# Steps 3 and 1 of a convolution kernel alternate in batches of four units in place of two, over all eight PSUM banks

## The chip, the cores and the metric

The kernel runs on one core of one Trainium2 chip. The metric is the device time of one execution in microseconds. A core has TensorE (matmuls, written PE; its weight loads are written PEld), VectorE (DVE), ScalarE (ACT), GpSimd (POOL) and SyncE (SP), which issues most DMAs. Matmuls write to PSUM, which the kernel uses as eight banks of 128 x 512 float32; ScalarE and VectorE copy or combine from there into SBUF.

## The reference

Two parts follow each other: a long convolution with a gate, and a soft mixture of experts over its output. The change lies in the convolution.

```python
def _attn_ref(x, v, pos_emb, w1, w2):          # x, v: (4, 11456, 128)
    h_filt = (np.maximum(pos_emb @ w1, 0.0) @ w2) * np.exp(-0.01 * pos)[:, None]
    u = x * v
    L = 2 * S
    Uf = np.fft.rfft(u, n=L, axis=1)
    Hf = np.fft.rfft(h_filt, n=L, axis=0)
    y = np.fft.irfft(Uf * Hf[None], n=L, axis=1)[:, :S, :]
    return x * y

def _moe_ref(x, phi, w1, w2):                  # x: the 45824 rows of the above
    logits = x @ phi                           # 8 experts x 4 slots
    d = softmax of logits over the rows;  slot_input = d.T @ x
    slot_out = relu(slot_input[e] @ w1[e]) @ w2[e]     for each expert e
    c = softmax of logits over the slots
    return c @ slot_out
```

## The kernel before

The transforms are done as matmuls with tables of cosines and sines, of length 111 x 197 in place of 2 x 11456. The 128 channels are cut into eight groups of 16 (`G = 8`, index `g`), and the 64 sequences of a group into 16 units of four (`NU = 16`, index `u`). A group goes through four steps:

- Step 1 (`first`, `first_out`): VectorE forms a unit's folded products of x and v (`p1_sd`, five instructions, in the place of the loaded x), TensorE multiplies them with `tab1x` on four quarters of its array at once (L138), and ScalarE copies two banks per unit into the tile `T` (L150).
- Step 2 (`p2`): matmuls of `T` with `W` into one bank (L279), a product with the filter's spectrum `Hs` on VectorE (L282), two sums on GpSimd back into `T`.
- Step 3 (`p3`): eight matmuls per unit of `T` with `tab3` (L296; the trace has two records for each), two banks per unit, and two ScalarE copies into the tile `E` (L302).
- Step 4 (`p4`, `p4_copy`, `p4_gate`, `p4_out`): matmuls of `E` with `tab4` into two banks (L331), two ScalarE copies, VectorE's sums and the gate with x, and DMAs to the scratch tensor.

The loop over `g` overlaps two groups. For `g` from 1 to 7 an iteration has two stages: first step 3 of group `g - 1` and step 1 of group `g` alternate, unit by unit; then step 4 of group `g - 1` and step 2 of group `g` do. Step 1 of a pair of units writes the part of `T` that step 3 of the same pair reads, so step 3 of a pair comes first. `inorder` and `steady` keep each engine's instructions in the order in which the code is written.

In the first stage (L385 to L412) the pairs `b` = 0 to 7 go: step 3 of units 2b and 2b + 1, then step 1 of the same units. In the first pair alone the matmuls of step 1 come ahead of step 3, and their copies behind. So step 3 of pairs 0 and 1 stand side by side, and step 1 of pairs 0 and 1 at the two sides of them. After each step 3 unit VectorE's `p1_sd` of the unit two further on is queued; after each step 1 unit the load of x six units further on (`p1_x`, into the place that this unit leaves, `ld` has 6). `p1_v` loads v. From the fourth pair on, loads of `Hs` for step 2 are put between.

PSUM is two pools of four banks. `psa` has four buffers of one bank, handed out in turn: step 1 takes two for a unit, step 2 one for each four columns. `pso` (tag `psb`) has two buffers of two banks: step 3 takes one for a unit, step 4 one for a block of rows. A buffer is taken again only when what was in it has been read.

```python
psa = ctx.enter_context(tc.tile_pool(name="psa", bufs=4, space=bass.MemoryType.PSUM))
pso.append(ctx.enter_context(tc.tile_pool(name="pso", bufs=2, space=bass.MemoryType.PSUM)))
```

Of the kernel before, what the change touches and what calls it, by code (L numbers as in the profile page):

```python
# [11 lines left out]
F32 = mybir.dt.float32  # L12
F32R = mybir.dt.float32r
AF = mybir.ActivationFunctionType
# [7 lines left out]
J = 99  # L22
# [3 lines left out]
R = 56  # L26
RP = 64
FO = 64
G = 8
# [32 lines left out]
def conv_part(ctx, tc, cp, moe, xf, vf, xi, xe, pos, w1, w2, win, t1x, t1h, wt, t3, t4, hs, scr):  # L62
# [64 lines left out]
        eng.tensor_tensor(out=hid[:, 0, rs], in0=hb[:, :, 0], in1=hb[:, :, 1], op=ALU.add)  # L127
        nc.vector.tensor_tensor(out=hid[:, 1, rs], in0=hb[:, :, 0], in1=hb[:, :, 1], op=ALU.subtract)

    def first(g, u, sd):  # L130

        ps = [psa.tile([128, 2, 2, J], F32, tag="psa", name=f"p1_{g}_{u}_{h}") for h in range(2)]
        for i in range(2):
            for s in range(2):
                for h in range(2):
                    js = slice(RP * h, RP * h + JH)
                    for d in range(2):
                        steady(g, nc.tensor.matmul(  # L138
                            ps[h][RP * d : RP * d + RP, i, s, :], lhsT=sd[js, i, s, d, :],
                            rhs=tab1x[js, J * (s + d) : J * (s + d + 1)],  # L140
                            start=True, stop=True, tile_position=(RP * h, RP * d)))
        return ps

    def first_out(g, u, ps):

        for h in range(2):
            dst = T[:, :, 2 * (u % 2) + h, u // 2]
            src = ps[h].rearrange("p c s k -> p s k c")
            if g or h == 0:
                steady(g, nc.scalar.activation(dst, src, AF.Copy))  # L150
            else:
                inorder(nc.vector.tensor_copy(out=dst, in_=src))
# [51 lines left out]
    def p1_v(g, u):  # L204
        k = u % HV if g == 0 else u - PRE
        if 0 <= k < HV:
            vt = Hs.rearrange("p k x -> p (k x)")[:, 8 * R * k : 8 * R * k + 8 * R]
        elif HV <= k < NU - 3:
            vt = m_half(g, k - HV)[:, : 8 * R]
        else:  # L210
            vt = ld.tile([128, 8 * R], F32, tag="lv", name=f"v_{g}_{u}", bufs=2)
        vt = vt.rearrange("p (c q r) -> p c q r", c=2, q=4)
        inorder(nc.sync.dma_start(out=vt, in_=vf[g, u]))
        vts[u] = vt

    def p1_x(g, u):
        if g == 0 and u < NU // 2:
            xt = moe.E[:, J * N1 + 8 * RP * u :][:, : 8 * RP].rearrange("p (c q r) -> p c q r", c=2, q=4)
        elif g == 0 and u >= NU - 2:
            xt = m_half(g, u).rearrange("p (c q r) -> p c q r", c=2, q=4)  # L220
        else:
            xt = ld.tile([128, 2, 4, RP], F32, tag="ld", name=f"x_{g}_{u}")
        inorder(nc.sync.dma_start(out=xt, in_=xf[g, u]))
        xts[u] = xt

    def p1_sd(g, u, eng):
        xt, vt = xts.pop(u), vts.pop(u)
        xr = xt[:, :, :, :R]
        inorder(eng.tensor_tensor(out=xr, in0=xr, in1=vt, op=ALU.mult))  # L229
        for m, op in ((0, ALU.add), (2, ALU.subtract)):  # L230
            inorder(eng.tensor_tensor(out=vt[:, :, m : m + 2], in0=xr[:, :, 0:2], in1=xr[:, :, 2:4], op=op))
        sd = xt.rearrange("p c (s d) r -> p c s d r", s=2)
        vq = vt.rearrange("p c (s q) r -> p c s q r", s=2)
        for d, op in ((0, ALU.add), (1, ALU.subtract)):
            inorder(eng.tensor_tensor(out=sd[:, :, :, d, :R], in0=vq[:, :, :, 0], in1=vq[:, :, :, 1],
                                      op=op))
        return sd
# [30 lines left out]
    for k in range(0, J, 4):  # L268
        filter_second(k)

    def p1(g, u, sd):
        first_out(g, u, first(g, u, sd))

    def p2(g, k0):
        n = min(KB, J - k0)
# [11 lines left out]
        inorder(nc.gpsimd.tensor_tensor(out=Ty[:, 0], in0=m[:, :n, 0, 0], in1=m[:, :n, 1, 1], op=ALU.subtract))  # L287
        inorder(nc.gpsimd.tensor_tensor(out=Ty[:, 1], in0=m[:, :n, 1, 0], in1=m[:, :n, 0, 1], op=ALU.add))  # L288

    def p3(g, u):  # L290
        ps = pso[0].tile([J, 2, 512], F32, tag="psb", name=f"p3_{g}_{u}")
        for k in range(2):
            pk = ps[:, k, : 8 * R].rearrange("p (i q r) -> p i q r", i=2, q=4)
            for i in range(2):
                for s in range(2):
                    inorder(nc.tensor.matmul(pk[:, i, 2 * s : 2 * s + 2, :].rearrange("p q r -> p (q r)"),  # L296
                                             lhsT=T[0:N1, s, 2 * k + i, u // 2, :, u % 2],
                                             rhs=tab3[:, 2 * R * s : 2 * R * (s + 1)],
                                             start=True, stop=True))
        for k in range(2):  # L300
            c = 4 * u + 2 * k
            inorder(nc.scalar.activation(  # L302
                E[:J, :, :, c : c + 2].rearrange("p r q c -> p q r c"),
                ps[:, k, : 8 * R].rearrange("p (i q r) -> p q r i", i=2, q=4), AF.Copy))

    AINV = pow(N1, -1, N2)

# [71 lines left out]
    for g in range(G + 1):  # L379

        if g == 0:
            for u in range(NU):
                p1(g, u, sds.pop(u))
        elif g < G:
            if not pso:  # L385
                first_ps.close()
                pso.append(ctx.enter_context(tc.tile_pool(name="pso", bufs=2, space=bass.MemoryType.PSUM)))
            for b in range(NU // 2):
                if b >= 4:
                    for k in range(11 * (2 * b - 8), min(J, 11 * (2 * b - 5 if b == 7 else 2 * b - 6)), 11):  # L390
                        inorder(nc.sync.dma_start(out=Hs[:, k : k + 11], in_=hs[g, :, k : k + 11]))
                us = (2 * b, 2 * b + 1)
                ps = {u: first(g, u, sds[u]) for u in us if b == 0}
                for u in us:
                    p3(g - 1, u)
                    if u + 2 < NU:
                        sds[u + 2] = p1_sd(g, u + 2, nc.vector)
                for u in us:
                    if b:
                        ps[u] = first(g, u, sds[u])  # L400
                    first_out(g, u, ps[u])
                    w = u + 6
                    if w < NU:
                        p1_x(g, w)
                    elif w < NU + PRE and g + 1 < G:
                        p1_x(g + 1, w - NU)
                if b == 0:
                    for w in range(PRE + HV, NU):
                        p1_v(g, w)
                if b == NU // 2 - 1 and g + 1 < G:  # L410
                    for w in range(PRE):
                        p1_v(g + 1, w)  # L412
        else:
            dead = moe.E[:, 8 * 4 * C : 16 * 4 * C]
            spare = ([sm.tile([128, PW], F32, tag="m", name=f"xl_{i}", bufs=3) for i in range(3)]
                     + [spare[i % 2] for i in (next(turns), next(turns))]
                     + [dead[:, PW * i : PW * i + PW] for i in range(2)])
            turns = count()
            xvs = [p4_load(g - 1, rb) for rb in ORDER[:5]]
            moe.weights()  # L420
            for u in range(NU):
                p3(g - 1, u)
            moe.places()
# [611 lines left out]
```

## Time and profile before

| | us |
|---|---|
| median of 3 runs (lowest, highest) | 955.26 (954.97, 956.76) |
| the profiled execution | 958.19 |
| its span, first to last instruction | 956.4 |
| TensorE busy in the span | 906.3 (95%) |
| TensorE weight loads busy | 818.2 (86%) |
| VectorE busy | 735.1 (77%) |
| ScalarE busy | 445.7 (47%) |
| GpSimd busy | 382.0 (40%) |
| mean granted TensorE clock | 0.977 |

An engine is busy while at least one of its instructions runs. Rows of the timeline give start, length, engine, line, operation, operands and count, and in brackets the idle time ahead of the row and what ended it; rows of the stretches give the busy time of each engine with the count of instructions, then the granted TensorE clock, the share of the DMA engines and GB/s. Names lose their numbers in the trace: `p` stands for the PSUM tiles of steps 1 to 4, so the line tells which step it is. Matmuls overlap: a record lasts about 0.26 us in step 3, while one starts every tenth of a microsecond. Seven of the eight groups (`g` = 1 to 7) have the stage that the change touches, of some 38 us each; group 4 lies at 391 to 475 us.

### The profile page before, as it was taken

Reading aid. Unit: us, or ns where it says so; the run is one execution under the profiler, and the core shown is the slowest. Engines: PE = TensorE matmul, PEld = TensorE weight load, DVE = VectorE, ACT = ScalarE, POOL = GpSimd, SP = SyncE. Lnnn points to the kernel's source line nnn. Section 1 sums busy time; section 2 is a strip of 40 time slices with the busy share of each in tenths; the row PEclk is TensorE's granted clock in tenths of the full one; section 3 lists DMA queues with packets and bytes.
Section 4 is the critical chain, followed back from the end, with each engine's and each line's share of the span. In section 5 each row is a group of like instructions: output and inputs, shape, how many; then the busy total and the mean of one; then the engine's idle time right before and its main releaser. Section 6 shows DMA issues by size and latency. Waiting matters only on the chain.

```text
span 956.4 us, 32999 instructions
## 1 busy us (share of the span) xinstructions
PE 906.3 (95%) x14042; PEld 818.2 (86%) x14042; DVE 735.1 (77%) x1282; ACT 445.7 (47%) x965; POOL 382.0 (40%) x582
## 2 busy tenths in 40 slices
PE   6999999999999999999999999999999979997992
PEld 6998989999999999999999999999999967774541
DVE  7936768699789879979978997998693248886671
ACT  0655437514711741571174157117414438885461
POOL 4001760292077028207702820760382007778700
PEclk9899999999999999999999999999999989999995
DMA  8923985457735735873573576457247787774499
GB/s 254 397 72 119 336 267 169 140 168 245 229 123 171 247 120 172 247 233 118 157 255 122 173 236 212 148 171 245 84 131 243 226 287 272 262 262 115 193 416 377
DMA packets 104239, 201.18 MB, mean 210 GB/s; under 512 B 14167, under 2 KB 65577, under 8 KB 100252
## 3 DMA queue, kind: packets, MB, share of 16 engines
q1 hardware_dynamic: 103806, 198.89, 63.0%
q8 instruction: 111, 1.82, 0.8%
q14 instruction: 36, 0.29, 0.1%
q10 hardware_dynamic: 254, 0.11, 0.0%
q0 software_dynamic: 32, 0.07, 0.0%
HBM read 139.12 MB, written 59.90 MB: 208 GB/s over the span
## 4 chain that ended last, share of the span: by engine, by line
PE 81%; POOL 6%; DMA 5%; ACT 2%; issue 2%; DVE 2%; SPq 0%; DVEq 0%; ACTq 0%
PE p L296 22%; PE p L279 19%; PE p L331 17%; PE p L138 10%; PE f L160 3%; PE f L170 2%; DMA hs<-E 2%; PE pw L875 2%; POOL E L654 2%; POOL hs L664 2%; DMA out_dram<-xreg 2%; PE fl L181 1%; POOL hs L662 1%; PE pt L559 1%; PE ct L730 1%
## 5 line engine op out<-in xcount | busy, mean ns | idle before, releaser
L287 POOL TENSOR_TENSOR T<-m 111x256 f32<-111x256 f32 (+1 forms) x200 | 147.4, 737 | 424.5 <-DVE m L282 424.5
L282 DVE TENSOR_TENSOR m<-p,T 111x1024 f32<-111x1024 f32 (+1 forms) x175 | 200.0, 1205 | 25.1 <-PE p L279 24.0
L296 PE MATMUL p<-tab,T 111*99 111x112 f32 x2048 | 212.1, 263 | 2.6 <-DVE E L356 1.6
L296 PEld LDWEIGHTS p<-tab,T 111*99 111x99 f32 x2048 | 201.8, 171 | 10.7 <-issue 2.7
L279 PE MATMUL p<-T,W 128*111 128x128 f32 x1584 | 194.7, 278 | 0.0
L279 PEld LDWEIGHTS p<-T,W 128*111 128x111 f32 x1584 | 183.0, 173 | 7.3
L340 ACT ACTIVATE vc<-p 128x416 f32<-128x416 f32 x112 | 51.8, 515 | 285.3 <-DVE p L345 192.5
L331 PE MATMUL p<-tab,E 99*64 99x104 f32 x3584 | 173.4, 254 | 1.8 <-ACT E L302 1.1
L331 PEld LDWEIGHTS p<-tab,E 99*64 99x64 f32 x3584 | 162.6, 137 | 9.7 <-issue 1.3
L302 ACT ACTIVATE E<-p 99x448 f32<-99x448 f32 x256 | 130.2, 574 | 84.9 <-PE p L296 84.9
L288 POOL TENSOR_TENSOR T<-m 111x256 f32<-111x256 f32 (+1 forms) x200 | 145.9, 730 | 0.0
L150 ACT ACTIVATE T<-p 128x396 f32<-128x396 f32 x240 | 102.3, 529 | 6.3 <-PE p L138 6.1
L138 PE MATMUL p<-tab1x,x 53*64 53x99 f32 x3776 | 96.4, 248 | 3.1 <-DVE m L282 1.6
L138 PEld LDWEIGHTS p<-tab1x,x 53*64 53x64 f32 x3776 | 84.5, 132 | 9.9 <-DVE m L282 1.8
L345 DVE TENSOR_TENSOR p<-p,vc 128x832 f32<-128x832 f32 x56 | 57.3, 1023 | 22.0 <-ACT vc L340 22.0
L560 ACT ACTIVATE xreg<-pt 128x512 f32<-128x512 f32 x90 | 48.4, 598 | 9.1 <-PE pt L559 8.9
L559 PE MATMUL pt<-ident,xreg 128*128 128x128 f32 x358 | 48.8, 281 | 3.8 <-DMA xreg<-scr 3.8
L654 POOL TENSOR_TENSOR E<-lt,mx 128x512 f32<-128x512 f32 (+1 forms) x23 | 23.6, 1026 | 65.0 <-ACT et L636 65.0
L229 DVE TENSOR_TENSOR x<-x,T 128x448 f32<-128x448 f32 x55 | 34.0, 619 | 19.5 <-DMA x<-in_xf_dram 15.1
L559 PEld LDWEIGHTS pt<-ident,xreg 128*128 128x128 f32 x358 | 40.8, 148 | 9.1 <-DMA xreg<-scr 4.0
L353 DVE TENSOR_TENSOR E<-p,E 128x824 f32<-128x824 f32 x46 | 46.8, 1016 | 1.6
L282 DVE TENSOR_TENSOR m<-p,E 111x1024 f32<-111x1024 f32 (+1 forms) x25 | 29.0, 1207 | 18.9 <-ACT E L186 12.9
(107 smaller groups left out, 973.6 us busy)
## 6 DMA issues: line engine op xcount, KB each, us to landing
x<-in_xf_dram SPq DMA_DIRECT2D x118, 256.0 KB, 4.5
out_dram<-xreg SPq DMA_DIRECT2D x21, 1024.0 KB, 12.8
E<-in_xi_dram SPq DMA_DIRECT2D x46, 412.0 KB, 3.6
scr<-E SPq DMA_DIRECT2D x84, 206.0 KB, 3.2
T<-in_vf_dram SPq DMA_DIRECT2D x65, 224.0 KB, 5.1
hs<-E SPq DMA_DIRECT2D x12, 1024.0 KB, 5.0
T<-hs SPq DMA_DIRECT2D x63, 176.0 KB, 3.5
mv<-in_vf_dram SPq DMA_DIRECT2D x42, 224.0 KB, 5.3
```

The costliest lines, as they stand in the source:

```text
L138: steady(g, nc.tensor.matmul(ps[h][RP * d : RP * d + RP, i, s, :], lhsT=sd[js, i, s, d, :], rhs=tab1x[js, J * (s + d) : J * (s + d + 1)], ...
L150: steady(g, nc.scalar.activation(dst, src, AF.Copy))
L279: steady(g, nc.tensor.matmul(ps[:, i].rearrange("p b c -> p (b c)"), lhsT=W[:, k0 + i, :], rhs=Tf[:, :, k0 + i, :], start=True, stop=True))
L282: inorder(nc.vector.tensor_mul(m[:, :n].rearrange("p k s e c i -> p k s (e c i)").rearrange("p k s (b c) -> p k s b c", c=CG), ps[:, :n].u ...
L287: inorder(nc.gpsimd.tensor_tensor(out=Ty[:, 0], in0=m[:, :n, 0, 0], in1=m[:, :n, 1, 1], op=ALU.subtract))
L288: inorder(nc.gpsimd.tensor_tensor(out=Ty[:, 1], in0=m[:, :n, 1, 0], in1=m[:, :n, 0, 1], op=ALU.add))
L296: inorder(nc.tensor.matmul(pk[:, i, 2 * s : 2 * s + 2, :].rearrange("p q r -> p (q r)"), lhsT=T[0:N1, s, 2 * k + i, u // 2, :, u % 2], rhs ...
L302: inorder(nc.scalar.activation(E[:J, :, :, c : c + 2].rearrange("p r q c -> p q r c"), ps[:, k, : 8 * R].rearrange("p (i q r) -> p q r i", ...
L331: inorder(nc.tensor.matmul(pv[RP * h : RP * h + RP, 2 * k + i, w, :], lhsT=E[:J, r, 2 - 2 * w + s, :], rhs=tab4[:, s, o : o + NJ], start=( ...
L340: inorder(nc.scalar.activation(vc[:, w], pv[:, :, 0, :], AF.Copy, scale=2.0 * w - 1.0))
L345: inorder(nc.vector.tensor_tensor(out=pw, in0=pw[:, 1:2].to_broadcast([128, 2, 4, NJ]), in1=vc, op=ALU.add))
L559: inorder(nc.tensor.transpose(pt[:, j, :], self.xt[i][:, k + j, :], self.ident))
```

## The change

Steps 3 and 1 now alternate in batches of four units. The units 0 to 3 keep their beginning: step 1's matmuls of units 0 and 1, step 3 of 0 and 1, their copies; then step 3 of 2 and 3 and step 1 of 2 and 3. Batches 1 to 3 are step 3 of four units, then step 1 of the same four. A new function `banks` gives either step two banks from either pool: one double buffer of `pso` (`large`), or two single ones of `psa`. Step 3 takes single ones for the first two units of a batch and a double one for each of the last two. Step 1 does the same, except that in the last batch it is the first two units that take the double ones. In the first four units step 3 takes double, double, single, single; step 1 single, single, double, double. The loads of `Hs` go out four ahead of batch 2's step 3 and five ahead of batch 3's, in place of two to three ahead of each of the last four pairs. VectorE keeps its order (`p1_sd`), and so do the loads of x and v among each other on SP.

```diff
--- before.py
+++ after.py
@@ -127,9 +127,15 @@
         eng.tensor_tensor(out=hid[:, 0, rs], in0=hb[:, :, 0], in1=hb[:, :, 1], op=ALU.add)
         nc.vector.tensor_tensor(out=hid[:, 1, rs], in0=hb[:, :, 0], in1=hb[:, :, 1], op=ALU.subtract)
 
-    def first(g, u, sd):
-
-        ps = [psa.tile([128, 2, 2, J], F32, tag="psa", name=f"p1_{g}_{u}_{h}") for h in range(2)]
+    def banks(g, u, name, large):
+        if large:
+            t = pso[0].tile([128, 2, 512], F32, tag="psb", name=f"{name}_{g}_{u}")
+            return [t[:, h] for h in range(2)]
+        return [psa.tile([128, 512], F32, tag="psa", name=f"{name}_{g}_{u}_{h}") for h in range(2)]
+
+    def first(g, u, sd, large=False):
+
+        ps = [t[:, : 4 * J].rearrange("p (c s k) -> p c s k", c=2, s=2) for t in banks(g, u, "p1", large)]
         for i in range(2):
             for s in range(2):
                 for h in range(2):
@@ -268,8 +274,8 @@
     for k in range(0, J, 4):
         filter_second(k)
 
-    def p1(g, u, sd):
-        first_out(g, u, first(g, u, sd))
+    def p1(g, u, sd, large=False):
+        first_out(g, u, first(g, u, sd, large))
 
     def p2(g, k0):
         n = min(KB, J - k0)
@@ -287,10 +293,10 @@
         inorder(nc.gpsimd.tensor_tensor(out=Ty[:, 0], in0=m[:, :n, 0, 0], in1=m[:, :n, 1, 1], op=ALU.subtract))
         inorder(nc.gpsimd.tensor_tensor(out=Ty[:, 1], in0=m[:, :n, 1, 0], in1=m[:, :n, 0, 1], op=ALU.add))
 
-    def p3(g, u):
-        ps = pso[0].tile([J, 2, 512], F32, tag="psb", name=f"p3_{g}_{u}")
+    def p3(g, u, large=True):
+        ps = [t[:J, : 8 * R] for t in banks(g, u, "p3", large)]
         for k in range(2):
-            pk = ps[:, k, : 8 * R].rearrange("p (i q r) -> p i q r", i=2, q=4)
+            pk = ps[k].rearrange("p (i q r) -> p i q r", i=2, q=4)
             for i in range(2):
                 for s in range(2):
                     inorder(nc.tensor.matmul(pk[:, i, 2 * s : 2 * s + 2, :].rearrange("p q r -> p (q r)"),
@@ -301,7 +307,7 @@
             c = 4 * u + 2 * k
             inorder(nc.scalar.activation(
                 E[:J, :, :, c : c + 2].rearrange("p r q c -> p q r c"),
-                ps[:, k, : 8 * R].rearrange("p (i q r) -> p q r i", i=2, q=4), AF.Copy))
+                ps[k].rearrange("p (i q r) -> p q r i", i=2, q=4), AF.Copy))
 
     AINV = pow(N1, -1, N2)
 
@@ -385,31 +391,45 @@
             if not pso:
                 first_ps.close()
                 pso.append(ctx.enter_context(tc.tile_pool(name="pso", bufs=2, space=bass.MemoryType.PSUM)))
-            for b in range(NU // 2):
-                if b >= 4:
-                    for k in range(11 * (2 * b - 8), min(J, 11 * (2 * b - 5 if b == 7 else 2 * b - 6)), 11):
-                        inorder(nc.sync.dma_start(out=Hs[:, k : k + 11], in_=hs[g, :, k : k + 11]))
-                us = (2 * b, 2 * b + 1)
-                ps = {u: first(g, u, sds[u]) for u in us if b == 0}
-                for u in us:
-                    p3(g - 1, u)
+            def third(us, larges):
+                for u, large in zip(us, larges):
+                    p3(g - 1, u, large)
                     if u + 2 < NU:
                         sds[u + 2] = p1_sd(g, u + 2, nc.vector)
+
+            def behind(u):
+                w = u + 6
+                if w < NU:
+                    p1_x(g, w)
+                elif w < NU + PRE and g + 1 < G:
+                    p1_x(g + 1, w - NU)
+
+            def spectrum(i0, i1):
+                for k in range(11 * i0, 11 * i1, 11):
+                    inorder(nc.sync.dma_start(out=Hs[:, k : k + 11], in_=hs[g, :, k : k + 11]))
+
+            ps = [first(g, u, sds[u]) for u in range(2)]
+            third(range(2), (True, True))
+            for u in range(2):
+                first_out(g, u, ps[u])
+                behind(u)
+            for w in range(PRE + HV, NU):
+                p1_v(g, w)
+            third(range(2, 4), (False, False))
+            for u in range(2, 4):
+                p1(g, u, sds[u], True)
+                behind(u)
+            for b in range(1, NU // 4):
+                if b > 1:
+                    spectrum(4 * b - 8, 5 * b - 6)
+                us = range(4 * b, 4 * b + 4)
+                third(us, (False, False, True, True))
                 for u in us:
-                    if b:
-                        ps[u] = first(g, u, sds[u])
-                    first_out(g, u, ps[u])
-                    w = u + 6
-                    if w < NU:
-                        p1_x(g, w)
-                    elif w < NU + PRE and g + 1 < G:
-                        p1_x(g + 1, w - NU)
-                if b == 0:
-                    for w in range(PRE + HV, NU):
-                        p1_v(g, w)
-                if b == NU // 2 - 1 and g + 1 < G:
-                    for w in range(PRE):
-                        p1_v(g + 1, w)
+                    p1(g, u, sds[u], (u % 4 < 2) if b == 3 else (u % 4 > 1))
+                    behind(u)
+            if g + 1 < G:
+                for w in range(PRE):
+                    p1_v(g + 1, w)
         else:
             dead = moe.E[:, 8 * 4 * C : 16 * 4 * C]
             spare = ([sm.tile([128, PW], F32, tag="m", name=f"xl_{i}", bufs=3) for i in range(3)]
```

How the change moves instructions on TensorE at the start of the stage, for `g` = 1; `p1_1_u` is step 1 of group 1, unit u (a further 0 or 1 is a single bank), `p3_0_u` step 3 of group 0, unit u. Before, from the last row of step 1's unit 1:

```order
L138 MATMUL p1_1_1_1_1624<-tab1x_74,x_1_1_1037 64x99 x2
L296 MATMUL p3_0_0_1641<-tab3_75,T_78 99x112 x8
L296 MATMUL p3_0_1_1657<-tab3_75,T_78 99x112 x8
L296 MATMUL p3_0_2_1692<-tab3_75,T_78 99x112 x8
L296 MATMUL p3_0_3_1708<-tab3_75,T_78 99x112 x8
L138 MATMUL p1_1_2_0_1724<-tab1x_74,x_1_2_1180 64x99 x2
L138 MATMUL p1_1_2_1_1725<-tab1x_74,x_1_2_1180 64x99 x2
```

Step 3 of units 0 to 3 goes through the two double buffers twice. In the change:

```order
L302 MATMUL p3_0_0_1641<-tab3_75,T_78 99x112 x8
L302 MATMUL p3_0_1_1657<-tab3_75,T_78 99x112 x8
L302 MATMUL p3_0_2_0_1692<-tab3_75,T_78 99x112 x4
L302 MATMUL p3_0_2_1_1693<-tab3_75,T_78 99x112 x4
L302 MATMUL p3_0_3_0_1709<-tab3_75,T_78 99x112 x4
L302 MATMUL p3_0_3_1_1710<-tab3_75,T_78 99x112 x4
L144 MATMUL p1_1_2_1726<-tab1x_74,x_1_2_1180 64x99 x16
L144 MATMUL p1_1_3_1747<-tab1x_74,x_1_3_1182 64x99 x16
L302 MATMUL p3_0_4_0_1768<-tab3_75,T_78 99x112 x4
L302 MATMUL p3_0_4_1_1769<-tab3_75,T_78 99x112 x4
```

Units 2 and 3 of step 3 now take the single banks, in turn those of `p1_1_0_0`, `p1_1_0_1`, `p1_1_1_0` and `p1_1_1_1`; step 1 of units 2 and 3 takes the double buffers; and step 3 of unit 4 follows, with units 5 to 7 behind it.

ScalarE at the same place, before:

```order
L302 ACTIVATE E_79<-p3_0_0_1641 99x4x56x2 x2
L302 ACTIVATE E_79<-p3_0_1_1657 99x4x56x2 x2
L150 ACTIVATE T_78<-p1_1_0_0_1605 128x2x198
L150 ACTIVATE T_78<-p1_1_0_1_1606 128x2x198
L150 ACTIVATE T_78<-p1_1_1_0_1623 128x2x198
L150 ACTIVATE T_78<-p1_1_1_1_1624 128x2x198
L302 ACTIVATE E_79<-p3_0_2_1692 99x4x56x2 x2
L302 ACTIVATE E_79<-p3_0_3_1708 99x4x56x2 x2
L150 ACTIVATE T_78<-p1_1_2_0_1724 128x2x198
L150 ACTIVATE T_78<-p1_1_2_1_1725 128x2x198
```

And in the change, to the same units:

```order
L308 ACTIVATE E_79<-p3_0_0_1641 99x4x56x2 x2
L308 ACTIVATE E_79<-p3_0_1_1657 99x4x56x2 x2
L156 ACTIVATE T_78<-p1_1_0_0_1605 128x2x198
L156 ACTIVATE T_78<-p1_1_0_1_1606 128x2x198
L156 ACTIVATE T_78<-p1_1_1_0_1623 128x2x198
L156 ACTIVATE T_78<-p1_1_1_1_1624 128x2x198
L308 ACTIVATE E_79<-p3_0_2_0_1692 99x4x56x2
L308 ACTIVATE E_79<-p3_0_2_1_1693 99x4x56x2
L308 ACTIVATE E_79<-p3_0_3_0_1709 99x4x56x2
L308 ACTIVATE E_79<-p3_0_3_1_1710 99x4x56x2
L156 ACTIVATE T_78<-p1_1_2_1726 128x2x198 x2
L156 ACTIVATE T_78<-p1_1_3_1747 128x2x198 x2
```

The order of the copies is the same; those of step 3's units 2 and 3 read two separate banks each.

TensorE at the last batch, before:

```order
L138 MATMUL p1_1_13_1_2131<-tab1x_74,x_1_13_1918 64x99 x2
L296 MATMUL p3_0_14_2153<-tab3_75,T_78 99x112 x8
L296 MATMUL p3_0_15_2164<-tab3_75,T_78 99x112 x8
L138 MATMUL p1_1_14_0_2175<-tab1x_74,x_1_14_1974 64x99 x2
L138 MATMUL p1_1_14_1_2176<-tab1x_74,x_1_14_1974 64x99 x2
```

And in the change:

```order
L302 MATMUL p3_0_14_2115<-tab3_75,T_78 99x112 x8
L302 MATMUL p3_0_15_2126<-tab3_75,T_78 99x112 x8
L144 MATMUL p1_1_12_2137<-tab1x_74,x_1_12_1897 64x99 x16
L144 MATMUL p1_1_13_2156<-tab1x_74,x_1_13_1918 64x99 x16
L144 MATMUL p1_1_14_0_2175<-tab1x_74,x_1_14_2010 64x99 x2
L144 MATMUL p1_1_14_1_2176<-tab1x_74,x_1_14_2010 64x99 x2
```

Behind step 3's units 14 and 15, which fill the double buffers, it was units 14 and 15 of step 1 that came, on single banks; now it is units 12 and 13, on the same two double buffers.

## The prediction

> **What bounds the kernel now.** I read the page first: engines, slices, costliest groups. TensorE's row is nine tenths or more from the second slice to the 32nd, and the groups that the change touches are steps 3 (L296) and 1 (L138) on TensorE and their copies out of PSUM on ScalarE (L302, L150).
>
> ```profile
> span 956.4 us, 32999 instructions
> PE 906.3 (95%) x14042; PEld 818.2 (86%) x14042; DVE 735.1 (77%) x1282; ACT 445.7 (47%) x965; POOL 382.0 (40%) x582
> PE   6999999999999999999999999999999979997992
> L296 PE MATMUL p<-tab,T 111*99 111x112 f32 x2048 | 212.1, 263 | 2.6 <-DVE E L356 1.6
> L302 ACT ACTIVATE E<-p 99x448 f32<-99x448 f32 x256 | 130.2, 574 | 84.9 <-PE p L296 84.9
> L150 ACT ACTIVATE T<-p 128x396 f32<-128x396 f32 x240 | 102.3, 529 | 6.3 <-PE p L138 6.1
> ```
>
> Here ScalarE waits for TensorE (84.9 us), not the reverse. Next, the table by stretches for one group: first the stage with steps 3 and 1, then the one with steps 4 and 2.
>
> ```profile
> 474.20:513.00 38.80, 38.69 (x772) 36.61 (x768) 31.51 (x80) 28.24 (x64) 0.39 (x1) 1.00 0.76 244
> 513.00:557.80 44.80, 44.80 (x655) 42.99 (x646) 42.20 (x45) 6.81 (x16) 34.15 (x50) 1.00 0.47 140
> ```
>
> The columns are length, then PE, PEld, DVE, ACT, POOL busy, clock, DMA. TensorE is busy for 38.69 of 38.80 us and for all of 44.80. So each microsecond of matmul time saved or of waiting added in the first stage moves the end by a microsecond, in each of seven groups.
>
> **Term 1: fewer changes between the steps.** Third, the timeline of a steady stretch in group 4, with two windows cut inside a step 1 block to read its pace.
>
> ```profile
> 413.61 1.61 PE L138 MATMUL p<-tab1x,x 53*64 53x99 f32 x64
> 415.15 3.31 PE L296 MATMUL p<-tab,T 111*99 111x112 f32 x32
> 418.40 1.61 PE L138 MATMUL p<-tab1x,x 53*64 53x99 f32 x64
> 419.94 3.31 PE L296 MATMUL p<-tab,T 111*99 111x112 f32 x32
> ```
> ```profile
> 414.26 0.96 PE L138 MATMUL p<-tab1x,x 53*64 53x99 f32 x36
> ```
> ```profile
> 403.99 0.61 PE L138 MATMUL p<-tab1x,x 53*64 53x99 f32 x20
> ```
> ```profile
> 392.15 6.72 PE L296 MATMUL p<-tab,T 111*99 111x112 f32 x64
> 393.75 0.15 DVE L356 TENSOR_TENSOR E<-p,E 128x4 f32<-128x4 f32 x1
> 394.02 4.67 PEld L296 LDWEIGHTS p<-tab,T 111*99 111x99 f32 x48 [0.27 <-issue]
> 395.84 1.02 ACT L302 ACTIVATE E<-p 99x448 f32<-99x448 f32 x2 [0.84 <-PE p L296]
> 396.74 1.67 ACT L150 ACTIVATE T<-p 128x396 f32<-128x396 f32 x4
> ```
>
> A batch of two units takes 419.94 - 415.15 = 4.79 us. Its pure work: step 3's pace is read from 48 weight loads in 4.67 us, one of them 0.17 long: 4.50 / 47 = 0.096 each, 32 make 3.06. Step 1: 36 rows take 0.96 and 20 rows 0.61, so 16 rows take 0.35, or 0.022 each; 64 make 1.40. Together 4.46, so a pair of changes (3 to 1 and back) costs 4.79 - 4.46 = 0.33 us, between 0.30 and 0.36 as the rounding of the two paces allows. Nothing waits in these batches, so it goes with the change itself. Before, a group has 7 blocks of step 3 among its step 1 blocks (units 0 to 3 already run together); after, 4. Three pairs go: 3 x 0.33 = 1.0 us per group, **7.0 us** in seven.
>
> **Term 2: units 2 and 3 of step 3 move to the single-bank pool.** Before, they take the double-bank buffers of units 0 and 1. After, they take the four single banks that step 1's units 0 and 1 fill at the group's start, and those are emptied on ScalarE only behind the copies of step 3's units 0 and 1. The second copy starts at 395.84, when unit 1's matmuls are over; the first copy of step 1 is this:
>
> ```profile
> 396.74 0.50 ACT L150 ACTIVATE T<-p 128x396 f32<-128x396 f32 x1
> ```
>
> It ends at 397.24. From an end elsewhere to TensorE's start the same group shows 0.12 us (DVE L356 ends at 393.90, weights start at 394.02), so unit 2 can start at 397.36. In before it starts 31 steps ahead of the block's last matmul, which starts at 392.15 + 6.72 - 0.26 = 398.61: 398.61 - 31 x 0.096 = 395.64. The wait is 1.72 us, with 0.03 to get back to pace 1.75; **12.2 us** in seven groups. Nothing covers it: TensorE has no other work in its order, and step 1's units 2 and 3 stand behind. Unit 2's second half needs the bank freed some 0.4 us later, while its first half takes 0.77; unit 3 needs the third bank (0.8 us later) 1.5 us later. So it is paid once a group.
>
> **Term 3: the last batch swaps its pools.** Step 1's units 12 and 13 now take the double-bank buffers that step 3's units 14 and 15 have just filled. The nearest rows are a step 3 block and the copies of its last unit:
>
> ```profile
> 400.34 3.32 PE L296 MATMUL p<-tab,T 111*99 111x112 f32 x32
> 402.16 1.03 ACT L302 ACTIVATE E<-p 99x448 f32<-99x448 f32 x2 [0.37 <-PE p L296]
> 403.59 1.61 PE L138 MATMUL p<-tab1x,x 53*64 53x99 f32 x64
> 403.70 1.05 ACT L302 ACTIVATE E<-p 99x448 f32<-99x448 f32 x2 [0.50 <-PE p L296]
> ```
>
> The two copies of the block's last unit end at 404.75, so unit 13 could start at 404.87; without a wait it starts half a step 1 block after 403.59, at 403.59 + 0.70 = 404.29. The wait is 0.58 us (0.45 to 0.65, as the copies start a little sooner or later), **4.1 us** in seven groups. Unit 12 has its buffer: the copies of the block's first unit end at 403.19, 0.4 us ahead of it. Step 4 behind finds unit 12's buffer long empty. The same copies in batches 1 and 2 fall on buffers needed over 1 us later.
>
> **What I cost at nothing, and its cover.** ScalarE: two copies of step 3 take 1.02 us (395.84) and four of step 1 take 1.67 (396.74), at most 1.9 us per unit of both steps against 2.3 of TensorE, so a block of four is emptied before its bank is due. The separate banks let step 3's copies start a half earlier; ScalarE has idle time there, so nothing. VectorE (L229 to L235, 2.0 us a unit) and the loads of x stand closer, since loads of units 10 to 13 are now released by four step 1 units in a row:
>
> ```profile
> 402.70 8.09 SPq L223 DMA_DIRECT2D x<-in_xf_dram  x6
> 408.06 0.63 DVE L229 TENSOR_TENSOR x<-x,T 128x448 f32<-128x448 f32 x1 [2.22 <-DMA x<-in_xf_dram]
> 410.06 0.62 DVE L229 TENSOR_TENSOR x<-x,mv 128x448 f32<-128x448 f32 x1
> 422.31 0.62 DVE L229 TENSOR_TENSOR x<-x,v 128x448 f32<-128x448 f32 x1
> 429.51 3.08 PE L331 MATMUL p<-tab,E 99*64 99x104 f32 x64
> 433.72 3.49 DVE L282 TENSOR_TENSOR m<-p,T 111x1024 f32<-111x1024 f32 x3 [2.13 <-PE p L279]
> ```
> ```profile
> x<-in_xf_dram SPq DMA_DIRECT2D x12, 256.0 KB, 5.5
> T<-hs SPq DMA_DIRECT2D x9, 176.0 KB, 3.8
> v<-in_vf_dram SPq DMA_DIRECT2D x3, 224.0 KB, 4.8
> ```
>
> Group 4 put on the new order: units 2 and 3 of step 1 end at 402.0, step 3 of units 4 to 7 at 408.4, their step 1 at 411.3, units 8 to 11 at 417.6 and 420.5, the rest at 426.9 and 430.4. Load 8 is issued at 402.7 as now, since seven loads of v stand ahead of it on SP; VectorE is through unit 9 at 410.06 + 2.0 = 412.1. Load 10 leaves SP when unit 4 is done, about 409.6, and lands 5.5 us later at 415.1; VectorE ends unit 10 at 417.1, unit 11 at 419.1; TensorE wants them at 419.2 and 419.9. It holds with 0.8 us to spare. SP carries the two more spectrum loads of batch 2 (T<-hs, 0.45 us each to issue) ahead of loads 14 and 15, which wait for unit 8 at 418.6 anyway. The last five spectrum loads are issued at 421, and step 2 wants them at 433. The next group's second v load waits for VectorE's unit 15, which ends at about 427.7 (now 422.31 + 2.0 = 424.3); with 4.8 us it lands at 432.5, and VectorE is through its unit at 434.5, while step 2's first product is due 4.2 us into step 4 (433.72 - 429.51), at 434.7. The two x input loads of step 4 are issued behind it, at 428.6, and wanted some 10 us later. If this cover fails, VectorE is late for step 2, whose four banks give another microsecond.
>
> **Sum.** +12.2 + 4.1 - 7.0 = +9.3 us. The profiled execution took 958.19 (span 956.4), 2.9 above the median of the runs; it would become 967.5. On the median 955.26 I predict **964.6 us**, 1.0% more.
>
> **Rivals.** B: the new wait halves TensorE's clock. The clock's rows come in windows of 3.41 us:
>
> ```profile
> 138.02:141.43 3.41, 1.49 (x34) 0.97 (x30) 2.63 (x4) 0.66 (x2) 2.42 (x4) 1.00 1.00 301
> 141.44:144.85 3.41, 3.39 (x18) 3.39 (x19) 3.31 (x9) 0.42 (x1) 0.00 (x0) 0.50 0.80 258
> 766.08:769.49 3.41, 1.75 (x40) 1.54 (x35) 2.08 (x4) 0.93 (x2) 0.00 (x0) 1.00 0.94 275
> 769.50:772.90 3.40, 1.28 (x6) 1.28 (x7) 1.44 (x3) 0.08 (x1) 0.00 (x0) 0.50 0.98 395
> 871.89:875.30 3.41, 1.91 (x45) 1.40 (x38) 2.23 (x8) 1.07 (x4) 3.10 (x7) 1.00 0.46 114
> 875.31:878.71 3.40, 2.42 (x25) 1.52 (x23) 1.40 (x8) 2.45 (x8) 3.40 (x4) 1.00 0.00 0
> ```
>
> A window with 1.49 or 1.75 us of TensorE busy is followed by one at clock 0.50; one with 1.91 is not. A wait of 1.72 leaves the matmul's end running 0.16 into it, so 1.56 us idle; wholly inside one window that leaves 1.85 busy, between the two bounds. It is wholly inside in (3.41 - 1.56) / 3.41 = 54% of positions, 3.8 of seven groups. A halved window costs 1.7 us (18 matmuls fit, as above, where 36 would). All told +6.5: 971.1, and up to 976.5 if every group is hit. The Trainium skill, TensorE: Matmul & The Clock Gate, section HAM oscillation, says that only gaps in TensorE's work above about 3.4 us bring the clock down. By that rule no wait here would cost clock and the sum would stay; the trace shows drops behind windows that were 44 and 51% busy, so the rule does not settle it.
>
> C: the input loads come late. If load 10 needs 7.5 us, unit 11 is 1.2 us late in each group: +8.4, 973.0. Against it: the loads that fill the queue now (v, seven in a row) are over by then. D: term 3 is hidden, if unit 15's copies start at once on an idle ScalarE and are shorter than 1.05: 960.5. E, the other side: unit 2 does not wait, because the single banks are handed out otherwise than in turn or emptied ahead of step 3's copies. It decides at 395.64: were step 1's first copy over by 395.5 and not 397.24, term 2 would be nil and the sum 4.1 - 7.0 = -2.9, 952.4. Against it: ScalarE's order has the two step 3 copies first, and the second of them cannot begin ahead of 395.84. F: gains and waits cancel, if a pair of changes costs 0.78 and not 0.33 us (16.3 / 21); the rows of term 1 leave no room for it.
>
> **How the numbers follow.** The forecast as it stands (two waits, own range 962 to 967): 0.62. B 0.15, C 0.05, D 0.08, E 0.06, F 0.04. A range from 959.5 to 972 holds the forecast, D and most of B; it leaves out E, F, the worst of B and C, about 0.18. Faster by over 0.2% (1.9 us, about what a measurement of this kernel can tell from no change) is E, 0.06, within it F, 0.04, slower the rest, 0.90.
>
> **What would show it.** In the profile after, each group has one TensorE idle of about 1.5 to 1.7 us ahead of step 3's unit 2, put down to ScalarE's T copy (L156), at seven places, some 11 us; a second of 0.4 to 0.6 ahead of step 1's unit 13, put down to ScalarE's E copy. A steady batch of four takes 9.58 - 0.33 = 9.25 us. The stage with steps 3 and 1 grows from 38.8 to about 40.1 us, the other stays at 44.8. The clock row tells B, and waits of VectorE for x or of TensorE for VectorE in the first stage tell C. I am wrong if the first wait is under 1 us.

## The result, and the profile after

The change makes the kernel slower. Its median is 965.41 us (964.65 to 966.38, 5 runs), that of the kernel before 956.76 (954.97 to 960.83, 5 runs); the ratio is 1.0088, with a 95% interval from 1.0061 to 1.0116. Measured a second time on another occasion (`e8_change_again`, below) the ratio was 1.0088 again, from 1.0060 to 1.0116. The forecast was 964.6. Two executions, one of the kernel before (2258 us) and one of `e6_loads_earlier` (3082 us), lie far outside all others and are left out of every figure below.

The page after: span, engines, TensorE's slices, then the groups of steps 3 and 1 and their copies (lines have moved by six: L302 is step 3, L144 step 1, L308 and L156 their copies).

```profile
span 962.9 us, 33019 instructions
PE 900.2 (93%) x14042; PEld 815.9 (85%) x14042; DVE 736.0 (76%) x1282; ACT 453.3 (47%) x965; POOL 382.0 (40%) x582
PE   6999999999999999999999999999999979997992
L302 PE MATMUL p<-tab,T 111*99 111x112 f32 x2048 | 208.7, 262 | 12.9 <-ACT T L156 10.3
L308 ACT ACTIVATE E<-p 99x448 f32<-99x448 f32 x256 | 138.2, 571 | 81.1 <-PE p L302 80.7
L144 PEld LDWEIGHTS p<-tab1x,x 53*64 53x64 f32 x3776 | 83.6, 132 | 10.0 <-ACT E L308 3.0
```

TensorE is busy for 6 us less and the span is 6.5 us longer. Step 3, which waited 2.6 us in all, now waits 12.9, of which 10.3 for ScalarE's copies of step 1. The slices show nothing of it: at 24 us a slice a wait of 1.7 us is lost in a 9. The list of waits, TensorE's own rows, counts them (total, times, longest):

```profile
PEld p L302 <- ACT T L156: 11.5, 7, 1.6
PE p L302 <- ACT T L156: 10.3, 7, 1.5
PEld p L144 <- ACT E L308: 3.0, 7, 0.4
```

Both come seven times, once a group. The first in group 4, in the timeline at the start of the stage:

```profile
396.13 3.65 PE L302 MATMUL p<-tab,T 111*99 111x112 f32 x32
399.82 1.00 ACT L308 ACTIVATE E<-p 99x448 f32<-99x448 f32 x2 [0.83 <-PE p L302]
401.25 3.32 PE L302 MATMUL p<-tab,T 111*99 111x112 f32 x32 [1.47 <-ACT T L156]
```
```profile
400.69 0.50 ACT L156 ACTIVATE T<-p 128x396 f32<-128x396 f32 x1
```

Units 0 and 1 of step 3 end at 399.78; ScalarE then copies unit 1 and only after it the first bank of step 1, which is free at 401.19; unit 2 starts at 401.25. From one start to the next TensorE loses 1.63 us, and 0.08 more on the second matmul, 1.71 in all. The second, at the last batch, with the steady batches ahead of it:

```profile
412.34 3.00 PE L144 MATMUL p<-tab1x,x 53*64 53x99 f32 x128
415.27 6.38 PE L302 MATMUL p<-tab,T 111*99 111x112 f32 x64
421.58 2.98 PE L144 MATMUL p<-tab1x,x 53*64 53x99 f32 x128
```
```profile
430.81 0.92 PE L144 MATMUL p<-tab1x,x 53*64 53x99 f32 x32
430.92 0.99 ACT L308 ACTIVATE E<-p 99x448 f32<-99x448 f32 x2 [0.51 <-PE p L302]
431.96 2.30 PE L144 MATMUL p<-tab1x,x 53*64 53x99 f32 x96 [0.23 <-ACT E L308]
434.18 2.01 PE L337 MATMUL p<-tab,E 99*64 99x104 f32 x40
```

Unit 15's copies end at 431.91 and unit 13 starts at 431.96. The last block of step 1 takes 434.18 - 430.81 = 3.37 us where an undisturbed one takes 415.27 - 412.34 = 2.93 (2.91 in the next): 0.46 lost. And a steady batch takes 421.58 - 412.34 = 9.24 us. The stages by the table, the same group as before:

```profile
478.90:518.50 39.60, 37.79 (x772) 36.17 (x768) 31.44 (x80) 29.34 (x64) 0.38 (x1) 1.00 0.75 245
518.50:563.20 44.70, 44.70 (x651) 42.99 (x646) 42.28 (x45) 6.80 (x16) 34.10 (x50) 1.00 0.42 124
```

I measure a first stage from the first matmul of step 1 to the first of step 4, by their starts in the timeline. Of groups 2 to 7 it took 38.43 to 38.89 us before and 39.58 or 39.59 after in each; the least, 38.43 and 39.58, are those with no other wait. The second stage is as it was, but for one wait of 0.7 us in group 2's. Other waits, in groups 4 to 6 above all, raise the mean before to 38.60, so in these two executions a group grows by 0.98 us, and the spans differ by 6.5 us and not by 7 x 1.15 = 8.1.

### The profile page after: what moved, and what is told of

It reads as the page before. It is cut to its first block, busy times and chain, and to the rows that moved or that the text cites. A ratio compares the mean times of both kernels' runs of the same rounds, so it can differ in the third digit from the quotient of the medians.

```text
span 962.9 us, 33019 instructions
## 1 busy us (share of the span) xinstructions
PE 900.2 (93%) x14042; PEld 815.9 (85%) x14042; DVE 736.0 (76%) x1282; ACT 453.3 (47%) x965; POOL 382.0 (40%) x582
## 4 chain that ended last, share of the span: by engine, by line
PE 79%; POOL 6%; DMA 5%; ACT 4%; issue 2%; DVE 2%; SPq 0%; DVEq 0%; ACTq 0%
PE p L302 21%; PE p L285 18%; PE p L337 17%; PE p L144 9%; PE f L166 3%; PE f L176 2%; DMA hs<-E 2%; PE pw L895 2%; POOL hs L684 2%; POOL E L674 2%; DMA out_dram<-xreg 2%; ACT E L308 2%; PE fl L187 1%; POOL hs L682 1%; PE pt L579 1%
## 5 line engine op out<-in xcount | busy, mean ns | idle before, releaser
L302 PE MATMUL p<-tab,T 111*99 111x112 f32 x2048 | 208.7, 262 | 12.9 <-ACT T L156 10.3
L302 PEld LDWEIGHTS p<-tab,T 111*99 111x99 f32 x2048 | 200.9, 171 | 19.1 <-ACT T L156 11.5
L308 ACT ACTIVATE E<-p 99x448 f32<-99x448 f32 x256 | 138.2, 571 | 81.1 <-PE p L302 80.7
L337 PE MATMUL p<-tab,E 99*64 99x104 f32 x3584 | 173.9, 255 | 2.3 <-ACT E L308 1.1
L337 PEld LDWEIGHTS p<-tab,E 99*64 99x64 f32 x3584 | 162.9, 137 | 10.2 <-issue 2.1
L156 ACT ACTIVATE T<-p 128x396 f32<-128x396 f32 x240 | 100.2, 523 | 9.5 <-PE p L144 9.4
L144 PE MATMUL p<-tab1x,x 53*64 53x99 f32 x3776 | 92.4, 247 | 4.1 <-DVE m L288 1.7
L144 PEld LDWEIGHTS p<-tab1x,x 53*64 53x64 f32 x3776 | 83.6, 132 | 10.0 <-ACT E L308 3.0
L579 PEld LDWEIGHTS pt<-ident,xreg 128*128 128x128 f32 x358 | 40.1, 146 | 9.2 <-DMA xreg<-scr 4.1
```

The lines of the kernel that those rows point to most:

```text
L144: steady(g, nc.tensor.matmul(ps[h][RP * d : RP * d + RP, i, s, :], lhsT=sd[js, i, s, d, :], rhs=tab1x[js, J * (s + d) : J * (s + d + 1)], ...
L308: inorder(nc.scalar.activation(E[:J, :, :, c : c + 2].rearrange("p r q c -> p q r c"), ps[k].rearrange("p (i q r) -> p q r i", i=2, q=4), ...
L337: inorder(nc.tensor.matmul(pv[RP * h : RP * h + RP, 2 * k + i, w, :], lhsT=E[:J, r, 2 - 2 * w + s, :], rhs=tab4[:, s, o : o + NJ], start=( ...
L579: inorder(nc.tensor.transpose(pt[:, j, :], self.xt[i][:, k + j, :], self.ident))
```

## Experiments

Three terms were to be told apart: the price of a pair of changes between steps 3 and 1, and the two waits. Kernels that were measured together share the runs of the kernel before (median 957.09 for `e1_double_first`, `e2_copies_first`, `e3_no_swap` and `e5_single_units`, 956.89 for the others). The ratio with its interval is estimated from all the runs, so it differs a little from the ratio of the medians.

### Both waits taken away

The batches of four stay; units 0 to 3 take their old pools, and in each batch both steps take the double buffers for the first two units.

```diff
-            third(range(2, 4), (False, False))
+            third(range(2, 4), (True, True))
             for u in range(2, 4):
-                p1(g, u, sds[u], True)
+                p1(g, u, sds[u])
...
-                third(us, (False, False, True, True))
+                third(us, (True, True, False, False))
...
-                    p1(g, u, sds[u], (u % 4 < 2) if b == 3 else (u % 4 > 1))
+                    p1(g, u, sds[u], u % 4 < 2)
```

> The changed kernel with other pools: units 0 to 3 keep the pools of the kernel before, and in every batch of four both steps take the double buffers for their first two units and the single banks for the last two. Batches of four stay. My theory (the two PSUM waits are the loss, 1.71 and 0.46 us per group in the profile after, and three pairs of changes per group gain 0.35 us each): both waits go, the gain stays alone, 7 x 1.05 = 7.4 us below the kernel before, ratio 0.992, and 15 us below the changed kernel; TensorE's idle time on ScalarE's copies ahead of steps 3 and 1 near nil. Rival 1 (the batches themselves gain nothing, the pace inside a block is what differs): level with the kernel before, 1.000. Rival 2 (loads of x released four at a time come late and hold VectorE): above 1.000, with TensorE waiting for VectorE in the first stage.

Measured: 952.81 us, ratio 0.9946 (0.9922 to 0.9969): faster than both kernels. The table by stretches for group 6:

```profile
554.90:592.30 37.40, 37.28 (x772) 36.08 (x768) 31.09 (x79) 28.93 (x63) 0.36 (x1) 1.00 0.77 245
```

The first stage takes 37.41 us where nothing disturbs it: 1.02 below the kernel before and 2.17 below the change, which is the two waits (1.71 + 0.46). The two rows of seven waits are gone. So the batches do gain, as expected per group; but the whole gained 4.3 us by the medians, 5.2 by the ratio, and not 7 x 1.02 = 7.1. Two things took some back in the profiled execution. Group 7 has a wait of TensorE at step 1's unit 11, in a stage where VectorE waits for loads of x:

```profile
DVE x L235 <- DMA x<-in_xf_dram: 4.6, 2, 2.4
PEld p L144 <- ACT T L156: 0.6, 1, 0.6
```

(the list names ScalarE; but VectorE's last product for unit 11 ends at 665.30, when the unit has just started at 665.10, where in the change it ends 0.9 to 3.5 us ahead). And a second stage took 45.75 in place of 44.76 us, with TensorE waiting 0.8 us for nothing that the trace names ("issue"). Whether these make up the rest is tried below.

### The first wait alone, from ScalarE's side

```diff
-            third(range(2), (True, True))
-            for u in range(2):
-                first_out(g, u, ps[u])
-                behind(u)
+            qs = []
+            for u in range(2):
+                qs.append(p3_mm(g - 1, u, True))
+                sds[u + 2] = p1_sd(g, u + 2, nc.vector)
+            for u in range(2):
+                p3_copy(g - 1, u, qs[u])
+                first_out(g, u, ps[u])
+                behind(u)
```

(`p3_mm` and `p3_copy` are the two halves of `p3`.)

> The changed kernel with one edit on ScalarE: at a group's start the two copies of step 1's unit 0 come ahead of the two copies of step 3's unit 1, not behind. Pools and TensorE's order as in the changed kernel. My theory (unit 2 of step 3 waits for step 1's first bank, which stands behind those two copies): the bank is free 0.89 us sooner, the wait falls from 1.71 to some 0.8 us per group, 6.2 us in all: about 2.4 us above the kernel before, ratio 1.0025. Rival (the wait has another source: split banks, the products of x and v, step 3's own inputs): no change against the changed kernel, ratio 1.009.

Measured: 954.83 us, ratio 0.9977 (0.9962 to 0.9991), below the kernel before and not above it. The wait did not halve, it went. ScalarE and TensorE at the start of group 4 (there at 389.06):

```profile
390.60 6.92 PE L305 MATMUL p<-tab,T 111*99 111x112 f32 x64
392.42 1.02 ACT L314 ACTIVATE E<-p 99x448 f32<-99x448 f32 x2 [2.32 <-PE p L305]
393.33 0.89 ACT L156 ACTIVATE T<-p 128x396 f32<-128x396 f32 x2
394.29 1.02 ACT L314 ACTIVATE E<-p 99x448 f32<-99x448 f32 x2
```

All 64 matmuls of units 0 to 3 are one block. Step 1's copies start at 393.33, right behind step 3's unit 0, while unit 1's matmuls still run; I had them wait for all of unit 1. In the code step 1's unit 0 writes only the parts of `T` that the first half of unit 1 reads. The bank is free at 393.83, ahead of need. The first stage takes 38.07 or 38.09, 1.50 less than in the change; the wait gave 1.71, and 0.2 comes back at unit 3, whose bank is now the late one (0.21 us from one start to the next there, in place of 0.096, and a slower second matmul). Two copies moved ahead of two others in ScalarE's order, with nothing else touched, turn the sign of this change. The second wait is there still:

```profile
PEld p L144 <- ACT E L314: 3.0, 7, 0.4
```

### The second wait alone

```diff
-                    p1(g, u, sds[u], (u % 4 < 2) if b == 3 else (u % 4 > 1))
+                    p1(g, u, sds[u], u % 4 > 1)
```

> The changed kernel without the swap of pools in the last batch: step 1's units 12 and 13 on single banks, 14 and 15 on double buffers, as in batches 1 and 2. My theory: unit 13's wait for step 3's copies (0.46 us per group) goes, and step 4's first matmuls wait instead for the copies of step 1's unit 14, 0.7 us by ScalarE's pace; some 1.7 us above the changed kernel in all, seen in the profile as seven waits of step 4 for ScalarE's T copy. Rival (that wait is nothing that comes from the swap): unit 13 waits as before, step 4 does not.

One execution, 961.31 us, whose time alone says little; its rows do. The list of waits:

```profile
PEld p L302 <- ACT T L156: 11.5, 7, 1.7
PEld p L337 <- ACT T L156: 4.9, 7, 0.7
```

Step 1's unit 13 waits no more, and step 4 (L337) waits 0.7 us in each of seven groups. The first stage takes 39.70 us, 0.12 more than in the change. So the wait does come from the swap of pools, and the swap is the lesser of two waits, though by 0.8 us in seven stages and not by the 1.7 expected.

### The price of a change, by more of them

The kernel before, with one unit of each step in turn from unit 2 on:

```diff
-            for b in range(NU // 2):
...
+            third(2)
+            third(3)
+            for u in range(2, NU):
...
+                p1(g, u, sds[u])
+                behind(u)
+                if u + 2 < NU:
+                    third(u + 2)
```

> The kernel before with more changes between the steps: from unit 2 on, one unit of step 1 and one of step 3 alternate, 13 blocks of step 3 in a group in place of 7; pools as before (step 3 double buffers, step 1 single banks). My theory (each pair of changes costs 0.35 us of TensorE time): 6 x 0.35 x 7 = 14.7 us above the kernel before, ratio 1.0154, no new waits. Rival (the extra time at a block's end is no price of the change but of something that comes once per pair of units, as copies or loads): level with the kernel before.

Measured: 971.58 us, ratio 1.0156 (1.0128 to 1.0183): 14.5 us, as expected. The table for group 5:

```profile
481.00:521.50 40.50, 40.39 (x772) 37.03 (x768) 30.44 (x77) 28.05 (x64) 0.38 (x1) 1.00 0.75 237
```

TensorE is busy in all of it: the price shows as busy time, not as waiting. That is why a profile with TensorE at 99% still held it.

### Batches of six

On `e1_double_first`, from unit 4 on:

```diff
-            for b in range(1, NU // 4):
...
+            due = 6
+            for b in range(2):
...
+                us = range(4 + 6 * b, 10 + 6 * b)
+                for i, u in enumerate(us):
+                    p3(g - 1, u, i % 4 < 2)
+                    if due in xts and due < NU:
+                        sds[due] = p1_sd(g, due, nc.vector)
+                        due += 1
...
+                for i, u in enumerate(us):
+                    p1(g, u, sds[u], i % 4 > 1)
+                    behind(u)
```

> As e1_double_first from the start to unit 3, then batches of six units: step 3 of units 4 to 9, step 1 of the same, then 10 to 15: 3 blocks of step 3 in a group in place of 4 (before: 7). The loads keep their order on SP, v ahead of x for units 8 and 9. My theory: one pair of changes less, 0.34 us per group, first stage 37.07 us if the loads hold, 9.5 us below the kernel before (0.990); but step 1's unit 9 now comes 0.5 us after VectorE's products for it, so in most groups TensorE waits some tenths for VectorE, and the stage ends between 37.1 and 38. Rival (the gain per pair ends at four): first stage 37.4 us or more with no wait for VectorE.

Measured: 956.14 us, ratio 0.9991 (0.9975 to 1.0007), no gain. Groups 2 and 3 have the first stage that the price foretells, 37.07 us:

```profile
305.65:342.70 37.05, 36.94 (x772) 35.98 (x768) 30.12 (x76) 28.13 (x63) 0.53 (x1) 1.00 0.72 240
```

In others it takes up to 39.71, with waits of 0.5 to 1.1 us, most at the fifth or sixth unit of a step 1 block, and five of six second stages are 0.5 to 1.3 us longer. VectorE now waits for loads, and step 2 for VectorE:

```profile
DVE x L235 <- DMA v<-in_vf_dram: 26.1, 6, 4.8
DVE x L235 <- DMA x<-in_xf_dram: 26.0, 11, 5.3
PEld p L144 <- ACT T L156: 4.3, 5, 1.1
PEld p L285 <- DVE m L288: 3.7, 4, 1.2
```

The first row is the load of v that waits for VectorE's last unit and reaches the next group's products late. It comes at unit 0 of each of groups 2 to 7, 3.9 to 4.8 us long. This is the cover that the prediction named, used up at six units. The list puts five waits of step 1 down to ScalarE, but in groups 4 to 7 unit 9 starts 0.2 us ahead of the end of VectorE's last product for it, as the late unit 11 did above; in groups 2 and 3 that product is over 0.1 and 1.4 us ahead. So those waits are for VectorE; one of the five, at 509.27 us, is of another kind, to which the next runs come.

### Loads of x ahead of loads of v

```diff
-            for w in range(PRE + HV, NU):
+            for w in range(PRE + HV, 12):
                 p1_v(g, w)
...
+            for w in range(12, NU):
+                p1_v(g, w)
             for b in range(1, NU // 4):
```

The second part stands behind step 1's units 2 and 3. On batches of four:

> The kernel with double buffers first (as in e1_double_first), and on SP the loads of x for units 8 and 9 come ahead of four of the seven loads of v (those for units 12 to 15), not behind all seven. My theory (what e1_double_first lost of its 7.1 us went to late loads of x: its profile has unit 11 of step 1 0.6 us late in one group, with VectorE waiting 2.2 us for load 8, and waits without a releaser): VectorE starts unit 8 about 1.5 to 2 us sooner, no step 1 unit waits for its products, every first stage takes 37.4 us, 7.1 us below the kernel before: ratio 0.9925. Rival (the loads cost nothing there; the loss is scatter between runs): as e1_double_first, 0.9946.

Measured: 951.68 us, ratio 0.9954 (0.9936 to 0.9973), the same as without the edit (0.9946). Five of groups 2 to 7 have the quiet 37.41 us, but group 4 has 38.27, and three second stages are 0.2 to 1.7 us longer, with these rows in place of the late loads (before, the first had 1.3 us in all):

```profile
PEld p L337 <- issue: 4.5, 6, 1.5
PE p L337 <- issue: 2.5, 2, 1.3
```

So late loads of x are not what keeps the gain of 7.1 us from this kernel. In groups 2 to 7 VectorE is through each unit 0.5 us or more ahead of TensorE here; most of what lengthens the stages of this execution is three waits of TensorE for which the trace names nothing ("issue"), of 0.9 to 1.6 us from one start to the next, 3.9 us in all.

The packets of the trace tell what these waits are. The page after has this row, and every other run has the same packets in this queue:

```profile
q8 instruction: 111, 1.82, 0.8%
```

Its packets are of 16 KB each, and 111 of them for TensorE's 28084 matmuls and weight loads make 253 to a packet. The first and second stages of groups 1 to 7 in the ten profiles hold 20 such waits of 0.4 us or more. In 19 of them TensorE stands 176 to 200 instructions past 253 times the number of packets landed so far, and the last packet landed 1.2 to 1.6 us ahead of its start (the twentieth is unit 9 of group 6 in `e4_batches_of_six`, which is for VectorE). The change's seven waits at unit 13, which are for ScalarE, stand anywhere from 16 to 224 past. So in these 19 waits TensorE had used up the instructions that had landed. There is 1 in the kernel before and none in `e5_single_units`; there are none to 3 with batches of four, and 2 and 6 with batches of six. Four units of step 1 use 256 instructions in 2.93 us, a whole packet, where step 3 uses 128 in 6.31; that this bunching is what makes the packets late is likely, but no run tried it alone.

On batches of six:

> Batches of six (as e4_batches_of_six) with the loads of x for units 8 and 9 ahead of four loads of v (as e6_loads_earlier). My theory: with the loads sooner, no waits; first stage 37.07 us in each group, 9.5 us below the kernel before, ratio 0.990. Rival: ScalarE cannot keep up with six step 1 units in a row, TensorE waits for its copies, and the stage is no shorter than with four (37.4 us).

Measured: 952.95 us, ratio 0.9965 (0.9943 to 0.9986). Groups 2 and 3 take 37.07, the others up to 38.68. VectorE still waits 27 us for v and 27 for x, but is through each unit of step 1 1.1 us or more ahead of TensorE in groups 2 to 7; the waits in the first stages of groups 4, 5 and 7 are four of the 19 for instructions, and step 2 waits 3.1 us for VectorE. It beats the kernel before, and not batches of four.

### The change once more

> The changed kernel as it is, on the same chip as the others. My theory: 7.8 us by its first stages (39.58 against 38.43 us), ratio 1.008; the two waits of 1.71 and 0.46 us in each group, as in its first profile. Rival (the first comparison was scatter): level with the kernel before.

Measured: 964.35 us, ratio 1.0088 (1.0060 to 1.0116), the first stage of groups 2 to 7 39.58 or 39.59 us, and the two waits in the same places, with the same lengths.

## Why the prediction was right

The direction, the size and the three terms held: +9.3 us forecast, +8.65 measured by the medians of the first comparison and +7.47 by those of the second. By the first stages it is 39.58 - 38.43 = 1.15 us a group, 8.1 in seven. That 964.6 lies only 0.8 below the measured 965.41 is in part luck: the sum was 1.3 us too high by the stages, and the kernel before came out 1.5 us slower in the comparison than the 955.26 that the forecast added it to. The stage was to grow to 40.1 us and took 39.58; 0.4 of that is a wait that the stage of 38.8 us had held before.

| term, us per group | forecast | measured | where |
|---|---|---|---|
| step 3's unit 2 waits for its single bank | +1.75 | +1.71 | timeline after |
| step 1's unit 13 waits for its double buffer | +0.58 | +0.46 | last block, 3.37 against 2.91 |
| three pairs of changes fewer | -1.00 | -1.02 | `e1_double_first`, 37.41 against 38.43 |

- Term 1. First stages without other waits take 40.50, 38.43, 37.41 and 37.07 us with 13, 7, 4 and 3 blocks of step 3: 0.345, 0.34 and 0.34 us a pair. That is a price proportional to the count over the whole range, where the forecast had 0.33 from one batch.
- Term 2. `e2_copies_first` shows the cause: it moves two copies on ScalarE and the wait goes. The forecast's 0.12 us from a copy's end to the matmul was too long; 401.19 to 401.25 is 0.06. The wait came out 0.04 shorter.
- Term 3 is the term that was mis-sized: 0.58 for 0.46. Two rows made it: the restart again (431.91 to 431.96 is 0.05, not 0.12), and copies of 0.99 us in place of 1.05. Its cause is shown by `e3_no_swap`.
- The covers held in the change: no wait of TensorE for VectorE in the first stages of groups 2 to 7. VectorE was through unit 11 2.9 us ahead of TensorE in group 4, where the forecast had 0.8, and 0.9 to 3.5 us in groups 2 to 7, so the cover was thicker than forecast. `e1_double_first`, where the stage is 2 us shorter, met unit 11 late in group 7, and `e4_batches_of_six` used the cover up at unit 9.
- Rival B, the halved clock, did not come. The stretch that holds the whole of group 4's wait and the next one:

```profile
398.10:401.50 3.40, 1.93 (x18) 1.75 (x19) 3.26 (x10) 2.56 (x7) 0.00 (x0) 1.00 0.95 344
401.52:404.90 3.38, 3.38 (x50) 3.27 (x51) 3.28 (x10) 2.80 (x7) 0.00 (x0) 1.00 0.59 133
```

  TensorE is busy for 1.93 of 3.40 us and the clock stays at 1.00. Before, stretches with 1.49 and 1.75 were followed by 0.50, and one with 1.91 was not, but such a bound does not hold: in the profile after, 2.16 us (138.68 to 142.09) is followed by 0.50, and 1.75 us (886.22 to 889.63) by 1.00. So the forecast's choice between 1.75 and 1.91 rested on too few rows, and why this wait cost no clock stays open. Here the rule of the Trainium skill (TensorE: Matmul & The Clock Gate, HAM oscillation), no TensorE idle gaps above some 3.4 us, agrees with what was measured, as the wait is of 1.5 us; it does not give the earlier drops.
- Rivals C to F fell: no load of x late enough to hold TensorE (VectorE waits 24.0 us for them in the whole execution, 15.8 before), both waits there, and a price of 0.34 and not 0.78 for a pair.
- The expectations that failed were of experiments. For `e2_copies_first` I took the copies to need all of unit 1's matmuls, read off the change's timeline, where ScalarE's order alone had put them there. The 7.1 us of `e1_double_first` came to 5.2 by the ratio, with 7.1 just inside the interval (its far end is 7.5 us), and `e4_batches_of_six`, `e6_loads_earlier` and `e7_six_loads_earlier` fell short of theirs, which lie outside their intervals.

## What to carry to other kernels

Two steps that use the matmul array in different tilings cost TensorE time here at each change between them, as busy time that no list of waits shows (that the tilings are the reason was not tried): measure a block's period, subtract its matmuls at their pace, and count the changes. Bigger batches save that, but only if each buffer they take has been emptied by then: for each block write down whose banks it takes, and where in the copying engine's order the copy stands that frees them, since one wait of 1.7 us ate five changes' worth. When such a wait shows up, look at the order of the copies and at which pool leads a batch before giving the batches up: either repair turned this change from 0.9% slower into 0.2 to 0.5% faster. And when TensorE waits for nothing that the trace names, count its instructions against the packets of the instruction queue that have landed.

## What the runs showed of the hardware

- A pair of changes between step 3 (111 x 99 weights) and step 1 (four quarters of 53 x 64) costs 0.34 us, the same in batches of one, two, four and six units. That it is proportional over the whole range was not expected.
- TensorE takes up a matmul 0.05 to 0.06 us after the end of the ScalarE copy that frees its bank (401.19 to 401.25, 431.91 to 431.96).
- TensorE can run out of landed instructions: 19 waits for which the trace names nothing, of 0.4 to 1.6 us from one start to the next, stand 176 to 200 instructions past 253 times the packets landed on q8, 1.2 to 1.6 us behind the last landing. The kernel before has one, of 0.47 us; `e7_six_loads_earlier` has six.
